# The first chunk's inverse: its store and its reload move from SyncE's DMA queue to ScalarE's

## The chip, the cores and the metric

The kernel runs on one core of a Trainium2 chip. The metric is the device time of one execution in microseconds (us), the median of several runs. A core has five engines that each work through their own instruction queue in order: TensorE (PE, matrix products; PEld is its weight load), VectorE (DVE), ScalarE (ACT), GpSimd (POOL) and SyncE (SP, which here only issues DMA transfers). A DMA transfer can be issued by more than one engine; the profile calls the issue SPq or ACTq, and lists the packets of SyncE's queue as q1 and those of ScalarE's as q10.

## The reference, cut to what matters

```python
def _attn_ref(q, k, v, beta):          # batch 4, heads 8, sequence 768, head size 48
    k_n = k / (np.linalg.norm(k, axis=-1, keepdims=True) + 1e-06)
    for t in range(S):
        kt, vt, bt = k_n[:, :, t], v[:, :, t], beta[:, :, t, None]
        y[:, :, t] = np.einsum('bhd,bhde->bhe', q[:, :, t], state)
        v_old = np.einsum('bhde,bhd->bhe', state, kt)
        state = state + bt[:, :, :, None] * np.einsum('bhd,bhe->bhde', kt, vt - v_old)

x = attention output as 3072 tokens x 384
h = x @ w_in                            # 384 x 2048
g = where(h >= 1, h, where(h <= -1, 0, (h + 1) ** 2 / 4))
x = g @ w_out                           # 2048 x 384
xn = x / rms(x) * rms_g                 # second block: gate and value 384 x 1536, silu, out
out = (silu(xn @ w_gate) * (xn @ w_val)) @ w_out2
```

All of it is in 32-bit floats.

## The kernel before, in words

The attention is computed in 12 chunks of 64 steps, with two pairs of batches per chunk. In a chunk the step-by-step recurrence becomes a triangular system, and its inverse is needed before the chunk's output. Chunk 0 has a short way of its own, `inv0` (lines 455 to 508): the Gram products `gk`, scaled, are stored to DRAM (`scr_a`, L449) and read back as 16 x 16 blocks, one block per partition (`nt`, eight loads, L473); VectorE inverts all blocks at once in 15 steps (`tmp` L479 and `x` L485) and copies the result, transposed, into `nt` (L487). That tile is stored to the DRAM scratch `scr` (L490) and reloaded in another layout as `c` (L493). VectorE multiplies `c` by a mask of coefficients `m` (L497) into the block-diagonal tile `dt` (L503). TensorE multiplies with `dt` (`tr`, L644 and L652) and goes on with products of 32 x 32 blocks (`tr`, L666).

Beside this start-up the kernel prepares the weights of the first block. They arrive as 64-bit floats in 32 tiles of 128 x 3,072 bytes (`wst`, issued by SyncE at L265). ScalarE converts each (`dy` L275, `da` L276), VectorE combines (`dy` L286, `da` L287, `w` L297), ScalarE copies the high part (`w` L300), TensorE forms the low part in three products (`wlo`, L315 to L317; the second and the third read the two parts of `w`), and ScalarE or VectorE copies it out (L320, L322). Later chunks use another routine, `inverse`, on GpSimd, whose store `scr_x` (L541) ScalarE issues. The two big blocks of matrix products (`hps`, `acc`, `gv`, L736 to L738) fill the rest of the time.

The order of all instructions is fixed when the program is built. Each step is a generator that yields stages (`S(engine, cost, needs, buffers)`), and a planner (`Flow`) picks which one is written next, by estimated times. The stages of the store and the reload are declared as stages of SyncE, so the planner places them by its clock for SyncE, and the instruction is written at that place in the program. Each engine then runs its own instructions in the order in which they were written. Where the planner expects TensorE to be idle, it writes a fixed number of small products (`warm`, L866). A DMA signals its end on one of eight semaphores, taken in turn; an instruction that uses the same one again waits for the transfer before.

Of the kernel before, what the change touches and what calls it, by code (L numbers as in the profile page):

```python
# [160 lines left out]
def kernel_body(  # L161
# [10 lines left out]
    nc = tc.nc  # L172
# [179 lines left out]
    inv = {}  # L352
# [5 lines left out]
    def bc(t, n):  # L358
        return t.unsqueeze(2).to_broadcast([t.shape[0], t.shape[1], n])

    def early(shape, name):
        n = int(np.prod(shape[1:]))
        t = wp.tile([128, 2, DM], F32R, name=name, tag="w")
        t = t.rearrange("p a b -> p (a b)").bitcast(F32)[:, 0:n]
        return t.rearrange("p (a b) -> p a b", b=shape[-1]) if len(shape) == 3 else t

    def half(b):
        return slice(64 * b, 64 * b + 64)
# [86 lines left out]
    def inv0():  # L455
        yield S("POOL", 2.0, (), ("tx", "tx", "z", "z", "wp"))
        off["m"] = moff = early([128, C], "moff")
        nc.gpsimd.memset(moff, -1.0)
        nc.gpsimd.memset(mdiag, -1.0)
        for b in range(2):  # L460
            for t, base, pat, cm in ((moff, -16, [[-16, 4], [0, 16]], 1), (mdiag, 0, [[-16, 4]], 1), (mdiag, 15, [[16, 4]], -1)):
                nc.gpsimd.affine_select(
                    out=t[half(b)], in_=t[half(b)], compare_op=ALU.is_ge, fill=0.0, base=base, pattern=pat, channel_multiplier=cm
                )
        x = p2.tile([128, 16, 16], F32, name="x0", tag="tx")
        nc.gpsimd.memset(x, 0.0)
        nc.gpsimd.affine_select(out=x, in_=x, compare_op=ALU.not_equal, fill=1.0, base=0, pattern=[[1, 16], [-1, 16]], channel_multiplier=0)
        yield S("SP", (5, 2.4), [("a_gram", 0, 2), ("a_gram", 1, 2)])
        nt = p2.tile([128, 16, 16], F32, name="nt0", tag="g21")
        for k in range(8):  # L470
            o, c = 16 * k, 16 * (k % 4)
            eng = nc.scalar if k in (1, 3, 5) else nc.sync
            eng.dma_start(out=nt[o:o + 16], in_=scr_a[0][o:o + 16, :, :, c:c + 16].rearrange("t u h s -> (u h) t s"))  # L473
        tmp = p2.tile([128, 64], F32, name="tmp0", tag="tx")
        for j in range(15):
            n, m = 15 - j, j + 1
            yield S("DVE", 0.37 + n * m * 2 / 960)
            tv = tmp[:, 0:n * m].rearrange("p (a b) -> p a b", a=n)
            nc.vector.tensor_tensor(  # L479
                out=tv,  # L480
                in0=nt[:, m:16, j:m].to_broadcast([128, n, m]),
                in1=x[:, j:m, 0:m].to_broadcast([128, n, m]),
                op=ALU.mult,
            )
            nc.vector.tensor_tensor(out=x[:, m:16, 0:m], in0=x[:, m:16, 0:m], in1=tv, op=ALU.add)  # L485
        yield S("DVE", 0.35)
        nc.vector.tensor_copy(nt, x.rearrange("p t s -> p s t"))  # L487
        yield S("SP", (1, 1.5))
        scr = dram.tile([16, 8, 2, H, 16], F32, name="scr_0", tag="scr_0")
        nc.sync.dma_start(out=scr.rearrange("s x u h t -> (x u h) s t"), in_=nt)  # L490
        yield S("SP", (1, 0.5))
        inv["c"] = p2.tile([128, 2 * H, 16], F32, name="c0", tag="z")
        nc.sync.dma_start(out=inv["c"], in_=scr.rearrange("s x u h t -> x s (u h t)"))  # L493
        yield S("DVE", 0.8, ["consts2"], ("x2",))
        m = p2.tile([128, 2 * H, 4], F32, name="m0", tag="g21")
        nn = coef[0][1].rearrange("p u h -> p (u h)")
        nc.vector.tensor_tensor(out=m, in0=bc(nn, 4), in1=mdiag.unsqueeze(1).to_broadcast([128, 2 * H, 4]), op=ALU.mult)  # L497
        inv[0] = x2p.tile([128, 2 * H, 4, 16], F32, name="dt", tag="x2")
        for u in range(2):
            us = slice(H * u, H * u + H)  # L500
            if u:
                yield S("DVE", 0.6, (), (), ("tx", "tx", "z", "z"))
            nc.vector.tensor_tensor(  # L503
                out=inv[0][:, us],
                in0=inv["c"][:, us].unsqueeze(2).to_broadcast([128, H, 4, 16]),
                in1=m[:, us].unsqueeze(3).to_broadcast([128, H, 4, 16]),
                op=ALU.mult,
            )
# [311 lines left out]
    def m1_rms(j):  # L820
# [38 lines left out]
        s=2, w_=2, g=4, acc=1, x2=1, ea=2,  # L859
# [13 lines left out]
    with tc.manual_schedule():  # L873
# [7 lines left out]
        fl.free["PE"] = 6.9  # L881
        fl.idle = spin
        fl.add(PG[0] + 6, inv0)
        for g, us in enumerate(GRP):
            p0 = PG[g]
# [189 lines left out]
```

## Time and profile before

| | |
|---|---|
| time, median of 3 runs | 1153.7 us (1152.92 to 1155.39) |
| profiled execution | 1154.3 us, span 1152.4 us |
| TensorE busy | 1107.5 us (96%) |
| VectorE busy | 661.8 us (57%) |
| ScalarE busy | 569.9 us (49%) |
| GpSimd busy | 286.3 us (25%) |
| SyncE's queue q1 | 141,536 packets, 132.31 MB |
| ScalarE's queue q10 | 23,440 packets, 2.93 MB |

The busy shares are averages over stages with different limits. The transfers that the change touches lie in the first 50 us, where TensorE runs short groups and warming products, and VectorE and ScalarE prepare weights. A timeline row gives start, length, engine, line and instruction; in brackets stands how long the engine sat idle before it and what ended that. Rows of the chain of waits give the work that the end of the program was traced back to.

### The profile page before, as it was taken

The numbers are of one execution on the slowest core, as the hardware profiler recorded it, in microseconds if no ns is written. First come the engines' busy times: TensorE is split into PE (matmuls) and PEld (weight loads), VectorE is DVE, ScalarE is ACT, GpSimd is POOL, SyncE is SP. The second block draws the span as 40 slices with busy tenths as digits, with TensorE's granted clock in tenths as the row PEclk, the third lists the DMA queues.
The fourth block names the chain that finished last, engine by engine and source line by source line (L and its number), as shares of the span: only waits on it lengthen the run. The fifth ranks groups of instructions, "written<-read, shape, count | busy, mean of one in ns | idle before, by whom it ended". The sixth has DMA issues, their size and how long they took to land.

```text
span 1152.4 us, 27191 instructions
## 1 busy us (share of the span) xinstructions
PE 1107.5 (96%) x11224; PEld 996.4 (86%) x11224; DVE 661.8 (57%) x1337; ACT 569.9 (49%) x1360; POOL 286.3 (25%) x479
## 2 busy tenths in 40 slices
PE   8979999999999999999999999999999999999998
PEld 7857888899998999899999999788888888888887
DVE  6797876786877876785775453443433333333333
ACT  4677877765765767567665464222212122122212
POOL 3282865858348114811000000000000000000000
PEclk9989999999999999999999999999999999999999
DMA  7945587784786556385440564001001010010000
GB/s 219 285 143 138 148 262 197 231 208 153 185 224 185 128 199 181 114 206 172 151 148 2 183 207 167 10 23 37 19 1 46 10 37 19 1 46 10 28 1 28
DMA packets 165099, 136.97 MB, mean 119 GB/s; under 512 B 115056, under 2 KB 126064, under 8 KB 164976
## 3 DMA queue, kind: packets, MB, share of 16 engines
q1 hardware_dynamic: 141536, 132.31, 38.2%
q10 hardware_dynamic: 23440, 2.93, 1.7%
q8 instruction: 88, 1.44, 0.5%
q14 instruction: 35, 0.29, 0.1%
HBM read 100.88 MB, written 34.34 MB: 117 GB/s over the span
## 4 chain that ended last, share of the span: by engine, by line
PE 74%; DVE 11%; ACT 4%; POOL 3%; DMA 3%; issue 2%; SPq 1%; DVEq 0%; POOLq 0%; ACTq 0%
PE acc L736 9%; PE gv L736 8%; PE gv L737 8%; PE gv L738 8%; PE acc L737 8%; PE acc L738 8%; PE hps L736 4%; PE hps L737 4%; PE hps L738 4%; PE gs L623 2%; POOL xi L536 2%; PE px L691 2%; POOL tmp L530 2%; PE tr L678 1%; DVE da L287 1%
## 5 line engine op out<-in xcount | busy, mean ns | idle before, releaser
L752 ACT ACTIVATE xh<-fix 128x512 fp32r<-128x512 f32 x72 | 45.5, 632 | 333.7 <-PE acc L738 328.4
L753 DVE TENSOR_TENSOR xl<-fix,xh 128x512 fp32r<-128x512 f32 x72 | 49.9, 694 | 270.6 <-ACT xh L752 270.6
L736 PE MATMUL hps<-xh,w 128*128 128x256 f32 x576 | 167.5, 291 | 9.9 <-DVE w__1065 L773 2.2
L737 PE MATMUL acc<-g,w 128*128 128x256 f32 x576 | 164.7, 286 | 10.6 <-DVE g L781 10.4
L736 PE MATMUL acc<-g,w 128*128 128x256 f32 x576 | 167.8, 291 | 2.7 <-ACT g L779 2.7
L736 PE MATMUL gv<-fix,w 128*128 128x512 f32 x432 | 168.2, 389 | 0.7 <-DVE fix L978 0.7
L737 PE MATMUL gv<-fix,w 128*128 128x512 f32 x432 | 168.1, 389 | 0.0
L738 PE MATMUL gv<-fix,w 128*128 128x512 f32 x432 | 168.1, 389 | 0.0
L737 PE MATMUL hps<-xl,w 128*128 128x256 f32 x576 | 164.2, 285 | 0.0
L738 PE MATMUL hps<-xh,w 128*128 128x256 f32 x576 | 163.9, 285 | 0.0
L738 PE MATMUL acc<-g,w 128*128 128x256 f32 x576 | 163.5, 284 | 0.0
L769 ACT ACTIVATE s<-hps 128x256 f32<-128x256 f32 x192 | 73.6, 384 | 108.3 <-PE hps L738 104.2
L736 PEld LDWEIGHTS hps<-xh,w 128*128 128x128 f32 x576 | 111.2, 193 | 13.7 <-DVE w__1065 L773 2.6
L737 PEld LDWEIGHTS acc<-g,w 128*128 128x128 f32 x576 | 110.7, 192 | 13.0 <-DVE g L781 12.9
L530 POOL TENSOR_TENSOR tmp<-nt,xi 128x87 f32<-128x87 f32 (+21 forms) x186 | 104.4, 561 | 54.5 <-DMA nt<-scr_a 40.4
L736 PEld LDWEIGHTS acc<-g,w 128*128 128x128 f32 x576 | 110.4, 192 | 6.1 <-ACT g L779 2.9
L536 POOL TENSOR_TENSOR xi<-xi,tmp 128x87 f32<-128x87 f32 (+21 forms) x186 | 110.4, 594 | 14.6
L737 PEld LDWEIGHTS hps<-xl,w 128*128 128x128 f32 x576 | 111.4, 193 | 0.3 <-DVE xl L732 0.3
L738 PEld LDWEIGHTS hps<-xh,w 128*128 128x128 f32 x576 | 111.3, 193 | 0.0
L738 PEld LDWEIGHTS acc<-g,w 128*128 128x128 f32 x576 | 110.7, 192 | 0.0
L770 ACT ACTIVATE s<-s,vhalf 128x256 f32<-128x256 f32 x192 | 97.9, 510 | 6.2
L736 PEld LDWEIGHTS gv<-fix,w 128*128 128x128 f32 x432 | 81.1, 188 | 17.8 <-DVE fix L978 1.1
(747 smaller groups left out, 2156.5 us busy)
## 6 DMA issues: line engine op xcount, KB each, us to landing
wst<-in_w SPq DMA_DIRECT2D x68, 384.0 KB, 4.6
w2d<-wst SPq DMA_DIRECT2D x36, 384.0 KB, 4.1
w<-w2d SPq DMA_DIRECT2D x36, 384.0 KB, 6.0
wsv<-in_w SPq DMA_DIRECT2D x36, 383.5 KB, 5.5
kvb<-in_kv SPq DMA_DIRECT2D x22, 384.0 KB, 5.5
kt<-in_kqT SPq DMA_DIRECT2D x24, 256.0 KB, 4.2
scr_a<-al SPq DMA_DIRECT2D x24, 256.0 KB, 3.9
qs<-in_kqT SPq DMA_DIRECT2D x48, 128.0 KB, 4.3
```

Source lines behind the costliest of these rows:

```text
L287: nc.vector.tensor_scalar(out=a, in0=yf, scalar1=0xFF800000, scalar2=None, op0=ALU.bitwise_and)
L530: nc.gpsimd.tensor_tensor(out=tv, in0=nt[:, m:32, j:m].to_broadcast([w, n, m]), in1=x[:, j:m, 0:m].to_broadcast([w, n, m]), op=ALU.mult,)
L536: nc.gpsimd.tensor_tensor(out=x[:, m:32, 0:m], in0=x[:, m:32, 0:m], in1=tv, op=ALU.add)
L623: nc.tensor.matmul(out=ps[half(b), h, 0:n], lhsT=kt[u][half(1 - b), 4 * k + h, :], rhs=qs[p][half(1 - b), b, 4 * k + h, 0:n], start=True, ...
L691: nc.tensor.matmul(out=ps[half(b), h, 0:D], lhsT=t[:, 0:C], rhs=v, start=True, stop=True)
L736: nc.tensor.matmul(out=out, lhsT=wh, rhs=xh, start=first, stop=False, skip_group_check=shared)
L737: nc.tensor.matmul(out=out, lhsT=wh, rhs=xl, start=False, stop=False, skip_group_check=shared)
L738: nc.tensor.matmul(out=out, lhsT=wl, rhs=xh, start=False, stop=last, skip_group_check=shared)
L752: nc.scalar.activation(out=hi, in_=src, func=ACTF.Copy)
L753: nc.vector.tensor_tensor(out=lo, in0=src, in1=hi.bitcast(F32), op=ALU.subtract)
L769: nc.scalar.activation(out=s, in_=ps, func=IDENTITY_SAT240, scale=240.0)
L770: nc.scalar.activation(out=s, in_=s, func=ACTF.Square, bias=vhalf, scale=1.0 / 480.0)
```

## The change

The two transfers are issued by ScalarE instead of SyncE. The stages keep their declaration as SyncE stages with the same costs, so the planner's order of all other instructions is the same.

```diff
         nc.vector.tensor_copy(nt, x.rearrange("p t s -> p s t"))
         yield S("SP", (1, 1.5))
         scr = dram.tile([16, 8, 2, H, 16], F32, name="scr_0", tag="scr_0")
-        nc.sync.dma_start(out=scr.rearrange("s x u h t -> (x u h) s t"), in_=nt)
+        nc.scalar.dma_start(out=scr.rearrange("s x u h t -> (x u h) s t"), in_=nt)
         yield S("SP", (1, 0.5))
         inv["c"] = p2.tile([128, 2 * H, 16], F32, name="c0", tag="z")
-        nc.sync.dma_start(out=inv["c"], in_=scr.rearrange("s x u h t -> x s (u h t)"))
+        nc.scalar.dma_start(out=inv["c"], in_=scr.rearrange("s x u h t -> x s (u h t)"))
```

On ScalarE's queue the two transfers now stand among the weight conversions, as the difference between the two programs shows (`scr_472` is the scratch, `c_558` the reloaded tile; in brackets what an instruction waits for, where `DMAHW` names a DMA semaphore):

```order
 L275 ACTIVATE dy<-wst 128x384 [waits DMAHW7_49,Activation_49]
 L276 ACTIVATE da_99<-wst 128x384
+L490 DMA scr_472<-nt_289 128x16x16 [waits DMAHW2_49,DMAHW5_49,DMAHW1_49,DMAHW6_49,DMAHW0_49,DVE_49]
 L275 ACTIVATE dy<-wst 128x384 [waits DMAHW0_49,Activation_49]
 L276 ACTIVATE da_100<-wst 128x384
@@ -39,4 +40,5 @@
 L276 ACTIVATE da_102<-wst 128x384
 L397 ACTIVATE n__545<-ss 128x16 [waits DVE_49]
+L493 DMA c_558<-scr_472 128x1x256 [waits DMAHW3_49]
 L300 ACTIVATE w<-dy 128x384 [waits DVE_49]
 L275 ACTIVATE dy<-wst 128x384 [waits DMAHW4_49,Activation_49]
```

The store stands behind the first of a run of four pairs of conversions, the reload behind the small `n_` and ahead of a `w` copy; its wait is for the store's semaphore.

On SyncE's queue, at the same place of the program, the weight loads close up:

```order
 L265 DMA wst<-in_w 128x384 [waits DMAHW2_49]
-L490 DMA scr_472<-nt_289 128x16x16 [waits DMAHW3_49,DVE_49]
 L265 DMA wst<-in_w 128x384 [waits DMAHW4_49]
 L265 DMA wst<-in_w 128x384 [waits DMAHW5_49]
 L265 DMA wst<-in_w 128x384 [waits DMAHW6_49]
-L493 DMA c_558<-scr_472 128x1x256 [waits DMAHW7_49,DMAHW3_49]
 L265 DMA wst<-in_w 128x384 [waits DMAHW0_49]
 L265 DMA wst<-in_w 128x384 [waits DMAHW1_49]
 L265 DMA wst<-in_w 128x384 [waits DMAHW2_49]
-L449 DMA scr_a_557<-al 128x512 [waits DVE_49]
+L449 DMA scr_a_557<-al 128x512 [waits DMAHW3_49,DVE_49]
```

Six loads move ahead of the places where the two transfers stood, and the store of `al` behind them now carries the wait for the semaphore of the moved store. The queues of TensorE, VectorE and GpSimd are the same as before.

## Rows read from the trace of the kernel before

**Rows 1.** Chain of waits, 14 to 62 us: start, length, what

```profile
39.66 0.23 DVE m L497
...
39.91 1.29 DVE dt L503 x2
...
44.86 0.87 PE tr L666 x32
```

**Rows 2.** Waits of SyncE's queue, 10 to 60 us: total, times, longest

```profile
SPq L493 <- DMA scr<-nt: 0.6, 1, 0.6
```

**Rows 3.** Timeline of SyncE's issues: start, length, queue, line, transfer

```profile
23.37 2.07 SPq L265 DMA_DIRECT2D wst<-in_w  x4
29.90 0.38 SPq L490 DMA_DIRECT2D scr<-nt  x1
...
33.91 0.69 SPq L493 DMA_DIRECT2D c<-scr  x1
```

**Rows 4.** Timeline of ScalarE, 28 to 45 us

```profile
30.35 0.55 ACT L275 ACTIVATE dy<-wst 128x384 f32<-128x384 f32 x1
...
34.36 0.22 ACT L397 ACTIVATE n__545<-ss 128x16 f32<-128x16 f32 x1 [0.61 <-DVE ss L391]
34.82 0.53 ACT L300 ACTIVATE w<-dy 128x384 fp32r<-128x384 f32 x1 [0.25 <-DVE dy L286]
```

**Rows 5.** DMA queues, 28.00 to 28.99 us: packets, MB, share of 16 engines

```profile
q1 hardware_dynamic: 145, 0.40, 100.4%
```

**Rows 6.** DMA packets by size, 30.75 to 30.99 us

```profile
DMA packets 113, 0.03 MB, mean 130 GB/s; under 512 B 105, under 2 KB 105, under 8 KB 113
```

**Rows 7.** DMA queues, 171.62 to 172.61 us

```profile
q1 hardware_dynamic: 147, 0.38, 96.5%
q10 hardware_dynamic: 145, 0.02, 11.9%
```

**Rows 8.** Timelines of ScalarE's and SyncE's issues around the second `scr_x` store

```profile
165.62 0.39 ACTq L541 DMA_DIRECT2D scr_x<-nt  x1
...
176.29 0.56 SPq L550 DMA_DIRECT2D tx<-scr_x  x1
```

**Rows 9.** DMA queues, 31.00 to 31.99 us

```profile
q1 hardware_dynamic: 1617, 0.16, 109.9%
```

**Rows 10.** Timeline of TensorE, 36 to 42 us and just before

```profile
35.97 0.81 PE L315 MATMUL wlo<-dy,ident 128*128 128x384 f32 x2
36.33 0.63 PE L316 MATMUL wlo<-w,ineg_r 128*128 128x384 f32 x1
...
36.97 2.84 PE L866 MATMUL warm<-ident 128*128 128x128 f32 x24
40.75 1.13 PE L644 MATMUL tr<-kvb,dt 64*64 64x48 f32 x32 [0.94 <-DVE dt L503]
41.69 0.52 PE L652 MATMUL tr<-dt,off 64*64 64x64 f32 x11
```

**Rows 11.** DMA issues of the whole span: transfer, times, KB, median us to landing

```profile
xn<-xn_d SPq DMA_DIRECT2D x18, 256.0 KB, 2.9
```

**Rows 12.** Timeline of TensorE: idle times of 2.0 to 2.5 us, in brackets

```profile
66.93 0.39 PE L736 MATMUL hps<-xh,w 128*128 128x256 f32 x1 [2.23 <-DVE w__1065 L773]
...
230.81 1.56 PE L623 MATMUL gs<-qs,kt 64*64 64x112 f32 x22 [2.48 <-DVE wt L585]
...
467.62 0.39 PE L736 MATMUL hps<-xh,w 128*128 128x256 f32 x1 [2.04 <-DVE w__7804 L773]
```

**Rows 13.** Stretches: length, busy time per engine, granted TensorE clock, DMA share, GB/s

```profile
68.00:70.00 2.00, 2.00 (x7) 1.39 (x6) 1.97 (x3) 1.00 (x3) 1.76 (x4) 0.51 0.03 11
70.00:72.00 2.00, 2.00 (x9) 1.14 (x10) 1.79 (x4) 1.70 (x4) 1.84 (x3) 0.64 0.00 0
...
232.00:234.00 2.00, 2.00 (x33) 2.00 (x32) 1.91 (x7) 0.01 (x1) 1.93 (x3) 0.50 0.65 103
...
468.00:470.00 2.00, 2.00 (x26) 1.70 (x24) 1.94 (x5) 0.91 (x3) 1.76 (x4) 1.00 0.98 301
```

## The prediction

> **What bounds the kernel now.** I read the chain of waits first, because it says which work the end hangs on. Over the whole span it is mostly TensorE, but in the first hundred microseconds it runs through VectorE's queue and then through short TensorE groups; the store and the reload stand in that part. The reader is to see in [rows 1] that `dt`, the instruction that uses the reloaded tile, starts at 39.91 us right behind `m` (39.66 us for 0.23 us): VectorE did not stop for the reload. So the reload is not late today, and an earlier reload buys nothing there. Four microseconds further on the chain is on TensorE (`tr` at 44.86 us), and TensorE is what I follow below.
>
> Then the waits of SyncE's queue and its issues. SyncE stood 0.6 us in front of the reload, until the store had landed [rows 2]. The store went out at 29.90 us; the reload at 33.91 us, which is therefore when the store had landed: 4.0 us [rows 3]. In front of the store SyncE stood from 25.44 us (four loads from 23.37 us, 2.07 us) to 29.90 us, for `nt`. Three weight loads were issued between the two transfers and three behind the reload.
>
> **Part 1, SyncE loses two waits.** The six weight loads no longer stand behind the store and the reload. The next ones may go from 25.4 us on [rows 3], as their own semaphores allow, instead of from 30.3 us, behind the store. Nothing on the chain waits for them: ScalarE takes the first of them only after the tile at 34.82 us [rows 4], and VectorE behind it runs without a stop [rows 1]. Value on the path: 0. But it fills the DMA engines at the very time of the store. In the trace the store's own small packets begin at about 30.75 us (105 of 113 packets in that quarter are under 512 B), so the older loads have drained by then [rows 6]. A saturated queue moved 0.40 MB in a microsecond [rows 5]; six loads of 128 x 3,072 B are 2.36 MB, so SyncE's queue now stays full for another 5.9 us, to about 36.6 us.
>
> **Part 2, the store on ScalarE's DMA queue.** ScalarE reaches it behind the second conversion, at 30.35 us, half a microsecond later than SyncE did, and `nt` is ready. The issue itself costs ScalarE some 0.4 us (the store took 0.38 us on SyncE [rows 3]), which lies in idle time: the conversions end well before `n_` at 34.36 us, and that one waits for VectorE [rows 4]. What matters is how the two queues share the DMA engines. The trace has such a stretch: between 171.62 and 172.61 us SyncE's queue (q1) was loaded with weight loads, and ScalarE's queue (q10) with the 128-byte packets of a `scr_x` store. q1 moved 147 packets and q10 145, one for one, whatever their size [rows 7]. That store was issued at 165.62 us, and the first transfer that needs it went out at 176.29 us [rows 8].
>
> The store is 128 x 16 runs of 64 B, 2,048 packets. Its first packets come about 1 us after its issue (0.85 us before, 29.90 to 30.75 us [rows 3, 6]), at 31.4 us. Up to 36.6 us, when the loads end, it gets one packet for each of theirs: 5.2 us x 145 = 750 packets. The other 1,300 then go at 1,617 per us [rows 9], 0.8 us, to 37.4 us. From the end of the bulk to the landing it was 1.8 us before (2,048 packets from 30.8 us at that rate end at 32.1 us; landed at 33.91 us). So it lands at about 39.2 us instead of 33.9 us. The bounds: 34.4 us if the store takes the 4.0 us it took, and 41.0 us, 30.36 + 10.7 us, if it takes what the store of [rows 8] took until its first user. I take 39.2 us, since the one-for-one row is the nearest to six loads in flight.
>
> **Part 3, the reload waits at the head of ScalarE's queue.** This is the new wait, and it is where I expect the loss. The reload stands behind `n_` (34.36 us) and in front of the `w` copy (34.82 us [rows 4]); everything ScalarE does is queued behind it: that copy, two pairs of conversions, the `wlo` copy, the two `z` copies. TensorE waits for the `w` copy: of the three matrix products into `wlo` the second (36.33 us) reads it [rows 10]. The reload goes at 39.2 us, takes 0.4 us to issue, and the copy starts at 39.6 instead of 34.82 us. It lasts 0.53 us, so the product can start at 40.15 instead of 36.33 us, 3.8 us late. Behind it stand 24 warming products in fixed order, which ended with 0.94 us to spare before `tr` [rows 10]: `tr` is 2.9 us late. The groups behind `tr` start 0.94 us apart by the length that its first one shows (40.75 to 41.69 us), the fourth would be through at 44.5 us, and the next `tr` began at 44.86 us [rows 1]: 0.4 us of cover. That leaves 2.5 us.
>
> Is the reload itself later than that? It landed by 39.91 us, 6.0 us after its issue at the latest [rows 1, 3]. With SyncE's queue drained I take 2.9 us, the nearest load in an otherwise quiet queue [rows 11]: landing at 42.1 us, `dt` 2.2 us late, half of it 0.7 us later still ahead of `tr` at 43.6 us. TensorE's path is the longer one.
>
> SyncE's next store of `al` also gains a wait, for the semaphore that the moved store counts on. It cannot leave before the moved store has landed, but then it meets an empty queue, which gives some of that back; it feeds GpSimd's first inverse, not the chain of [rows 1], and I put it at 0.
>
> **Part 4, the clock of TensorE.** The wait opens a gap on TensorE from about 36.6 us (end of the first `wlo` product) to 40.15 us: 3.5 us. Gaps of 2.23 and 2.48 us were followed by half clock, one of 2.04 us was not [rows 12]. After the first, the granted clock was 0.51 and 0.64 over two stretches of 2 us: 1.96 and 1.44 us at 1.2 GHz, 3.4 us in all; after the second it was 0.50, after the gap of 2.04 us it was 1.00 [rows 13]. Here such a stretch would cover the second `wlo` product, the third and the 24 warming ones, some 3.5 us of work at full clock, so it costs half its length, 1.7 us.
>
> **Sum.** 2.5 + 1.7 = 4.2 us. The chain downstream has no place where a fixed shift is absorbed (a wait on a transfer there is for one issued late too), so I carry it whole. The profiled execution took 1154.3 us around a span of 1152.4 us; that is 0.6 us above the median of 1153.7 us. 1154.3 + 4.2 = 1158.5 us for a profiled run, 1157.9 us for the median.
>
> **Rivals.**
> *No half clock.* TensorE was busy all the time before this gap, and the gap of 2.04 us passed. Then 2.5 us: 1156.2 us, just over 0.2%.
> *A second low stretch* after the first, as TensorE's later groups also wait on each other: another 1.7 us, 1159.6 us.
> *The store is not held up.* ScalarE would have its answer by 34.4 us, before the reload's turn comes, the copy would be 0.4 us late, inside the cover; 1153.7 us, no difference. For it speaks that the reload has only 128 long rows and the store is small; against it [rows 7]. It decides where the store lands: the `w` copy may be late by 1.0 us (TensorE came to it only at 36.33 us, the copy was done at 35.35 us) and by the 0.94 us of the warming products, so up to a landing at about 36.3 us nothing is lost, and the 0.4 us of cover takes that to 36.7 us. From there each microsecond costs one. The Trainium skill, page "DMA: Bandwidth & Descriptors", section "Issuing engines are not separate DMA queues", says that transfers issued by different engines run on the same 16 DMA engines and that another issuer saves only the time of issuing. By that rule alone the move would be worth nothing, 1153.7 us; [rows 7] show the sharing but also that the queue in which a small-packet store stands decides what it is interleaved with.
> *Faster.* The half-clock stretches of [rows 12, 13] hang on short gaps, and loads that come sooner might close two of them: 2 x 1.7 us, 1150.3 us without the loss of part 3. Nothing in the trace says that those gaps wait for loads: VectorE ends all three of [rows 12].
>
> **How the numbers follow.** Forecast 0.48; no half clock 0.18; a second low stretch 0.07; store not held up 0.21; faster 0.06. 0.2% is 2.3 us, about what a measurement of this kernel can tell from no change. Slower by more: all of the forecast, the second stretch, and half of the no-half-clock case, 0.64. Within: the store not held up and the other half, 0.30. Faster 0.06. The range goes from 1153.0 us, which takes in the store that is not held up, to 1159.5 us, which leaves out the second stretch and the gains.
>
> **What would show it.** In the profile after: the reload issued on ScalarE near 39 us (before 36.7 us would refute part 3, and the landing estimate of part 2 with it); q1 and q10 moving equal packet counts from 32 to 36 us; a gap of over 3 us on TensorE before the second `wlo` product; a granted clock below 1.00 around 40 to 44 us; `tr` near 45 us instead of 40.75 us. The prediction is wrong if the store's packets get more than their one-for-one share, or if a shift of some microseconds at 45 us has vanished by the time the TensorE-bound part begins.

## The result and the profile after

With the two transfers on ScalarE's queue the kernel takes 1160.6 us, the median of 7 runs (1159.75 to 1165.4). The kernel before took 1155.5 us on the same occasions (7 runs, 1152.92 to 1157.23). The ratio is 1.0054, with an interval from 1.0036 to 1.0071: slower by half a per cent. The profiled execution took 1160.43 us around a span of 1158.1 us; the one before was 1154.3 around 1152.4 us. The span has grown by 5.7 us.

The page of the kernel after, its busy times and its two DMA queues (packets, MB, share of 16 engines):

```profile
PE 1112.5 (96%) x11224; PEld 1001.7 (86%) x11224; DVE 660.0 (57%) x1337; ACT 569.5 (49%) x1360; POOL 288.3 (25%) x479
...
q1 hardware_dynamic: 139336, 132.05, 38.1%
q10 hardware_dynamic: 25640, 3.20, 1.9%
```

About 2,200 packets have moved from q1 to q10, the store's and the reload's; the engines have the same number of instructions as before, and all busy times but TensorE's stand within 2 us of those before. So what has changed is when things run. The chain of waits, 30 to 60 us, in order of time (start, length, what), shows it at once:

```profile
29.50 10.18 DMA scr<-nt
...
39.70 1.21 ACTq L493
...
40.95 0.53 ACT w L300
...
41.53 0.69 PE wlo L316
...
42.54 4.19 PE warm L866 x24
```

Before, this stretch of the chain ran over VectorE's `m` and `dt` [rows 1]. Now it begins with ten microseconds of the store, goes over the issue of the reload on ScalarE, the `w` copy behind it, and the `wlo` product that reads the copy.

SyncE's issues, 20 to 60 us (start, length, queue, line, transfer), to be read beside [rows 3]:

```profile
22.68 10.36 SPq L265 DMA_DIRECT2D wst<-in_w  x10
39.74 0.80 SPq L449 DMA_DIRECT2D scr_a<-al  x2
```

Four loads, the store, three loads, the reload and three loads have become ten loads in one piece. The store of `al`, which now counts on the moved store's semaphore, goes right after that one has landed (39.70 us).

ScalarE, 28 to 50 us, to be read beside [rows 4]:

```profile
29.50 0.39 ACTq L490 DMA_DIRECT2D scr<-nt  x1
...
39.70 1.21 ACTq L493 DMA_DIRECT2D c<-scr  x1
40.95 0.52 ACT L300 ACTIVATE w<-dy 128x384 fp32r<-128x384 f32 x1 [6.77 <-issue]
```

The store is issued 0.4 us earlier than before (29.50 for 29.90 us) and lands 5.8 us later (39.70 for 33.91 us). From the end of the small `n_` (33.96 us for 0.22 us) ScalarE stands at the reload, at the head of its queue, for 5.5 us, and the `w` copy comes 6.1 us late (40.95 for 34.82 us). The 6.77 us in brackets are put down to the engine's own issuing; they hold the reload's wait for the store and its 1.21 us of issue.

TensorE, 28 to 62 us, beside [rows 1, 10], and VectorE's `dt`:

```profile
35.57 0.81 PE L315 MATMUL wlo<-dy,ident 128*128 128x384 f32 x2
41.53 0.69 PE L316 MATMUL wlo<-w,ineg_r 128*128 128x384 f32 x1 [5.14 <-ACT w L300]
...
42.33 4.39 PE L866 MATMUL warm<-ident 128*128 128x128 f32 x24
46.65 1.14 PE L644 MATMUL tr<-kvb,dt 64*64 64x48 f32 x32
...
50.53 0.87 PE L666 MATMUL tr<-z,y 32*32 32x48 f32 x32
```

```profile
43.40 1.29 DVE L503 TENSOR_TENSOR dt<-c,m 128x512 f32<-128x512 f32 x2 [3.92 <-DMA c<-scr]
```

TensorE was idle for 5.14 us in front of L316, and the warming products then took 4.39 us instead of 2.84 us. VectorE waited 3.92 us for the reloaded tile, which it had not done before. The first of the 32 x 32 products (L666) starts at 50.53 instead of 44.86 us: 5.67 us, the growth of the span. Stretches of two microseconds (the last three columns are granted clock, DMA share and GB/s) tell why the warming products are long:

```profile
38.00:40.00 2.00, 0.00 (x0) 0.00 (x0) 1.41 (x4) 0.00 (x0) 0.00 (x0) 0.69 0.04 6
40.00:42.00 2.00, 0.47 (x1) 0.47 (x2) 0.00 (x0) 1.05 (x3) 0.00 (x0) 0.50 0.70 214
42.00:44.00 2.00, 2.00 (x10) 2.00 (x10) 0.60 (x1) 1.87 (x5) 0.00 (x0) 0.50 0.97 346
44.00:46.00 2.00, 2.00 (x13) 2.00 (x12) 1.93 (x5) 0.92 (x3) 0.00 (x0) 0.61 0.91 264
```

The clock fell to its lower level (1.2 GHz) while TensorE was idle and was back at 2.4 GHz shortly before `tr`. It fell once more from about 56 us on, which the part on the prediction comes back to.

Last, the packets of the two queues, one answer per microsecond. From 33.00 to 33.99 us:

```profile
q1 hardware_dynamic: 129, 0.35, 87.9%
q10 hardware_dynamic: 228, 0.01, 15.8%
```

From 34.00 to 34.99 us:

```profile
q10 hardware_dynamic: 1342, 0.09, 93.1%
q1 hardware_dynamic: 57, 0.14, 45.9%
```

From 36.00 to 36.99 us:

```profile
q1 hardware_dynamic: 138, 0.37, 94.9%
q10 hardware_dynamic: 50, 0.00, 3.5%
```

The microsecond before these, 32.00 to 32.99 us, has 153 packets of q1 and none of q10, although the store was issued at 29.50 us. So the store does three things in turn: it waits 3.6 us without a packet (the first one is at 33.12 us), it sends most of its 2,048 packets in a burst in which q1 falls to less than half of its rate, and its remainder trickles out beside the loads until 38.9 us.

### The profile page after: what moved, and what is told of

It is laid out like the page before. It is cut to its first block, busy times and chain, and to the rows that moved or that the text cites. A ratio compares the mean times of both kernels' runs of the same rounds, so it can differ in the third digit from the quotient of the medians.

```text
span 1158.1 us, 27193 instructions
## 1 busy us (share of the span) xinstructions
PE 1112.5 (96%) x11224; PEld 1001.7 (86%) x11224; DVE 660.0 (57%) x1337; ACT 569.5 (49%) x1360; POOL 288.3 (25%) x479
## 4 chain that ended last, share of the span: by engine, by line
PE 75%; DVE 12%; ACT 6%; DMA 3%; issue 2%; SPq 1%; POOL 0%; ACTq 0%; DVEq 0%; POOLq 0%
PE acc L736 9%; PE acc L737 8%; PE gv L736 8%; PE gv L738 8%; PE gv L737 8%; PE acc L738 8%; PE hps L736 5%; PE hps L737 4%; PE hps L738 4%; PE gs L623 2%; PE tr L678 1%; ACT al L445 1%; PE px L691 1%; DVE da L287 1%; DVE g L781 1%
## 5 line engine op out<-in xcount | busy, mean ns | idle before, releaser
L736 PE MATMUL hps<-xh,w 128*128 128x256 f32 x576 | 167.8, 291 | 9.3 <-DVE w__7804 L773 2.1
L737 PE MATMUL acc<-g,w 128*128 128x256 f32 x576 | 164.8, 286 | 7.8 <-DVE g L781 7.6
L736 PE MATMUL acc<-g,w 128*128 128x256 f32 x576 | 167.7, 291 | 3.0 <-ACT g L779 3.0
L736 PE MATMUL gv<-fix,w 128*128 128x512 f32 x432 | 168.2, 389 | 0.7 <-DVE fix L978 0.7
L737 PE MATMUL gv<-fix,w 128*128 128x512 f32 x432 | 168.1, 389 | 0.0
L737 PE MATMUL hps<-xl,w 128*128 128x256 f32 x576 | 164.2, 285 | 0.0
L736 PEld LDWEIGHTS hps<-xh,w 128*128 128x128 f32 x576 | 111.4, 193 | 13.4 <-DVE w__7804 L773 2.4
L737 PEld LDWEIGHTS acc<-g,w 128*128 128x128 f32 x576 | 110.8, 192 | 10.0 <-DVE g L781 9.7
L536 POOL TENSOR_TENSOR xi<-xi,tmp 128x87 f32<-128x87 f32 (+21 forms) x186 | 113.0, 608 | 14.6
L736 PEld LDWEIGHTS acc<-g,w 128*128 128x128 f32 x576 | 110.4, 192 | 6.4 <-ACT g L779 3.2
L737 PEld LDWEIGHTS hps<-xl,w 128*128 128x128 f32 x576 | 111.6, 194 | 0.0
L736 PEld LDWEIGHTS gv<-fix,w 128*128 128x128 f32 x432 | 81.1, 188 | 17.8 <-DVE fix L978 1.1
```

The source lines that it names most:

```text
L536: nc.gpsimd.tensor_tensor(out=x[:, m:32, 0:m], in0=x[:, m:32, 0:m], in1=tv, op=ALU.add)
L736: nc.tensor.matmul(out=out, lhsT=wh, rhs=xh, start=first, stop=False, skip_group_check=shared)
L737: nc.tensor.matmul(out=out, lhsT=wh, rhs=xl, start=False, stop=False, skip_group_check=shared)
```

## The experiments

Each edit is against the kernel after. The ratio is against the kernel before, on the same chip and occasion. The time at which `nt` is finished varies by about 2 us from run to run, so durations are compared rather than clock times; L666 is the first 32 x 32 product, which starts 15.4 us behind the start of the `nt` copy in the kernel before (29.49 to 44.86 us). Where an expectation names a theory by a letter, that letter stands for what the expectation says with it. The order is that of the questions: which of the two transfers costs, on which path, what holds the store up, and what the clock adds.

**The store alone.** The reload is back on SyncE's queue.

```
-        nc.scalar.dma_start(out=inv["c"], in_=scr.rearrange("s x u h t -> x s (u h t)"))
+        nc.sync.dma_start(out=inv["c"], in_=scr.rearrange("s x u h t -> x s (u h t)"))
```

> Only the store goes to ScalarE's queue; SyncE keeps the reload, and with it stops behind three more weight loads instead of six until the store has landed. Theory A (the loss comes from six loads ahead of the store, and is passed on because ScalarE stands at the reload): the store has three loads ahead (1.18 MB, 3 us), lands near 36.5 us instead of 39.7 us, the reload lands by 40 us, `dt` starts within 1 us of 39.9 us, ScalarE's `w` copy is on time at about 34.8 us, no gap over 2 us on TensorE at 36 to 42 us; time as before, ratio 0.999 to 1.002. Theory L (a store issued by ScalarE is slow in itself): the store still lands near 39.7 us, `dt` is 3 to 4 us late, ratio to before 1.003 to 1.005.

Measured: 1.0019, interval 1.0004 to 1.0033. ScalarE issued the store at 30.37 us. SyncE's loads and reload, then TensorE's `tr`:

```profile
24.21 5.21 SPq L265 DMA_DIRECT2D wst<-in_w  x7
...
37.93 0.70 SPq L493 DMA_DIRECT2D c<-scr  x1
```

```profile
41.79 1.23 PE L644 MATMUL tr<-kvb,dt 64*64 64x48 f32 x32 [2.22 <-DVE dt L503]
```

Seven loads are now ahead of the reload instead of ten, since SyncE itself stops at it. The store took 7.6 us (30.37 to 37.93 us) instead of 4.0, its first packet came at 33.74 us, and the `w` copy was on time (34.79 us). Counted from the `nt` copy (29.25 us), `dt` and `tr` were 1.3 us late, and the gap of 2.22 us in front of `tr`, which I had not expected, was followed by half clock; L666 came 2.6 us late. Moving the store alone is enough to starve it. The loss is less than half, but two things differ from the kernel after: ScalarE does not stand at the reload, and three loads fewer run ahead. The reload from GpSimd, below, shows that the first alone does not save the time.

**The reload alone.** The store is back on SyncE's queue.

```
-        nc.scalar.dma_start(out=scr.rearrange("s x u h t -> (x u h) s t"), in_=nt)
+        nc.sync.dma_start(out=scr.rearrange("s x u h t -> (x u h) s t"), in_=nt)
```

> Only the reload goes to ScalarE's queue; the store stays on SyncE, where it holds the loads back until `nt` is written. Theory A: the store lands at 33.9 us as before, before ScalarE comes to the reload at 34.4 us; ScalarE loses only the issue (0.7 to 1.2 us), inside the cover of 1.9 us, TensorE has no gap; ratio 0.999 to 1.001. Rival (a transfer issued by ScalarE costs its engine more than the issue): the `w` copy starts later than 36.7 us and `tr` is late by what goes beyond; ratio above 1.002.

Measured: 1.0032, 1.0019 to 1.0046. The reload on ScalarE, then TensorE's `tr`:

```profile
34.22 1.19 ACTq L493 DMA_DIRECT2D c<-scr  x1
```

```profile
43.25 1.95 PE L644 MATMUL tr<-kvb,dt 64*64 64x48 f32 x32 [3.64 <-DVE dt L503]
```

That the time would be as before fell. The store was as quick as ever and the reload was issued at 34.22 us, as early as on SyncE; the `w` copy at 35.46 us was within its cover. But six loads now went out of SyncE's queue in one piece from 30.12 us on, around the reload, and it sent its first packet at 38.34 us, 4.1 us after its issue, and landed 8.2 us after it. VectorE waited 2.73 us for it, TensorE 3.64 us for VectorE. So the reload starves in ScalarE's queue as the store does.

**The reload from GpSimd.** GpSimd is idle here, so nothing stands behind the reload.

```
-        nc.scalar.dma_start(out=inv["c"], in_=scr.rearrange("s x u h t -> x s (u h t)"))
+        nc.gpsimd.dma_start(out=inv["c"], in_=scr.rearrange("s x u h t -> x s (u h t)"))
```

> Store on ScalarE's queue as in the changed kernel, reload on GpSimd's queue, which has nothing to do from 22 to 48 us: the store is as late as in the changed kernel (39 to 40 us) but ScalarE does not stand in front of the reload. Theory A (ScalarE's standing is what costs): the `w` copy is on time near 34.5 us, the `wlo` products and the warming products behind them too, TensorE's gap shrinks to the wait for `dt` (from about 39.5 to 44 us); `tr` 3 to 4 us late instead of 5.9 us, ratio 1.002 to 1.004. Theory B (the late reload alone makes the loss): `dt` and `tr` as late as in the changed kernel, ratio 1.005.

Measured: 1.0052, 1.0032 to 1.0071. GpSimd's issue and TensorE's `tr`:

```profile
41.70 0.79 POOL L493 DMA_DIRECT2D c<-scr  x1 [20.32 <-DMA scr<-nt]
```

```profile
47.16 1.94 PE L644 MATMUL tr<-kvb,dt 64*64 64x48 f32 x32 [7.40 <-DVE dt L503]
```

ScalarE was free: the `w` copy came at 35.72 us and L316 on time. The loss was the same. The store took 11.3 us, `dt` waited 6.27 us for the reload, and TensorE stood 7.40 us for `dt`. So freeing ScalarE does not save the time: the path over the reload and `dt` alone is as long.

**The reload later in ScalarE's queue.** It is written one stage later, behind the `w` copy; both transfers stay on ScalarE.

```
-        nc.scalar.dma_start(out=inv["c"], in_=scr.rearrange("s x u h t -> x s (u h t)"))
         yield S("DVE", 0.8, ["consts2"], ("x2",))
+        nc.scalar.dma_start(out=inv["c"], in_=scr.rearrange("s x u h t -> x s (u h t)"))
```

> Both transfers on ScalarE's queue as in the changed kernel, loads ahead as there, but the reload is written six ScalarE instructions further on, behind the `w` copy that TensorE waits for. So ScalarE does not stand in front of that copy, and the reload still goes out when the store lands, near 39.7 us. Theory B (the late reload alone costs as much as ScalarE's standing): the `wlo` products are on time at 36.3 us, `dt` starts near 43.4 us as in the changed kernel, TensorE waits from 39.6 to 44.2 us and falls to half clock there; the first 32 x 32 `tr` near 50 us, ratio 1.004 to 1.0055. Theory of the forecast (ScalarE's standing is the longer path, the reload alone costs 2.2 us and no half clock): ratio 1.001 to 1.0025.

Measured: 1.0055, 1.0036 to 1.0074. ScalarE, then TensorE:

```profile
33.29 0.52 ACT L300 ACTIVATE w<-dy 128x384 fp32r<-128x384 f32 x1
...
39.10 1.21 ACTq L494 DMA_DIRECT2D c<-scr  x1
```

```profile
43.22 1.95 PE L644 MATMUL tr<-kvb,dt 64*64 64x48 f32 x32 [4.93 <-DVE dt L503]
```

This says the same without another engine: the copy and L316 (34.80 us) are on time, and TensorE's gap has moved from L316 to `tr`, where it is 4.93 us long and is followed by half clock in `tr` itself (1.95 us where the kernel before took 1.13). Two paths of nearly equal length start at the store's landing; taking one away leaves the other.

**The loads held until `nt` is finished.** SyncE stores 1 KB of `nt` to a spare place where the store used to stand, so it stops there until `nt` is finished, as in the kernel before, and then issues its loads. The 1 KB is an extra transfer.

```
         nc.scalar.dma_start(out=scr.rearrange("s x u h t -> (x u h) s t"), in_=nt)
+        nc.sync.dma_start(out=dram.tile([1, 16, 16], F32, name="hold", tag="hold"), in_=nt[0:1])
```

> Both transfers on ScalarE's queue as in the changed kernel, but SyncE first stores 1 KB of `nt` to a scratch of its own at the place where the whole store stood, so that the six loads cannot run ahead of the store. Theory A1 (the store lost because its packets share the DMA engines one for one with loads in flight): five or six loads are issued within 3 us of the store, so it shares with them and lands at 37 to 38.5 us; ScalarE stands at the reload until then, ratio 1.002 to 1.004. Theory A2 (the store's packets only come after the loads that were issued before it): nothing is ahead of it now, it lands at 34 to 35 us, no gap on TensorE, ratio 0.999 to 1.001. Theory L (ScalarE's issue itself): as in the changed kernel, 39.7 us, ratio 1.005.

Measured: 1.0036, 1.0017 to 1.0054. SyncE's loads behind the extra store, and ScalarE's reload:

```profile
30.57 9.63 SPq L265 DMA_DIRECT2D wst<-in_w  x6
```

```profile
39.88 1.20 ACTq L493 DMA_DIRECT2D c<-scr  x1
```

The packets from 31.00 to 31.49 us, and from 36.00 to 36.49 us:

```profile
q10 hardware_dynamic: 389, 0.02, 50.6%
q1 hardware_dynamic: 17, 0.04, 25.4%
```

```profile
q1 hardware_dynamic: 71, 0.21, 105.3%
q10 hardware_dynamic: 8, 0.00, 1.1%
```

With the earlier loads nearly through (84 packets of q1 from 30.25 to 30.99 us), the store (issued at 30.23 us) sent its first packet 0.9 us later, and over 800 packets before 32 us. Then the loads that were issued right behind it came in, and it landed only at 39.88 us, 9.65 us after its issue. The landing times of theories A1 and A2 did not come out. That of theory L, 39.7 us, did, so this run by itself leaves open that a store issued by ScalarE is slow in itself; the next one settles it. What the packets show is that the store went out at once and slowed when the loads came: loads issued after the store delay it too, by sharing, and for longer than an even one-for-one sharing would.

**The loads held until the store has landed.** Where the store used to stand, SyncE reads 1 KB of the scratch back, and so waits for the store.

```
         nc.scalar.dma_start(out=scr.rearrange("s x u h t -> (x u h) s t"), in_=nt)
+        nc.sync.dma_start(out=dram.tile([1, 256], F32, name="hold", tag="hold"), in_=scr[0:1, 0].rearrange("s u h t -> s (u h t)"))
```

> Both transfers on ScalarE's queue; SyncE reads 1 KB of the scratch back at the place where the store stood, so that it goes on with the loads only when the store has landed. The store then has a quiet queue, the reload has the loads of about 1 us ahead of it and the others behind. Theory A (loads in flight make the two late): the store lands 4.0 us after its issue as it did on SyncE's queue, 33.5 to 34.2 us; ScalarE does not stand, the `w` copy is at 35.5 to 36 us, inside its cover, the second `wlo` product on time at 36.3 us; the reload lands at 38.5 to 41 us, `tr` 0 to 1.5 us late, no or one short low stretch of the clock; ratio 1.000 to 1.003, the upper end if the loads, 3 us later than before, are missed later on. Theory L (ScalarE's issue is slow in itself): store at 38 us or later.

Measured: 1.0043, 1.0028 to 1.0058, more than I had expected. ScalarE's two transfers; then TensorE; then a piece of the chain of waits:

```profile
30.61 0.39 ACTq L490 DMA_DIRECT2D scr<-nt  x1
...
34.67 1.33 ACTq L493 DMA_DIRECT2D c<-scr  x1
```

```profile
40.13 1.14 PE L644 MATMUL tr<-kvb,dt 64*64 64x48 f32 x32 [0.21 <-DVE dt L503]
...
44.25 0.87 PE L666 MATMUL tr<-z,y 32*32 32x48 f32 x32 [0.17 <-DVE y L660]
...
49.22 2.47 PE L666 MATMUL tr<-z,y 32*32 32x48 f32 x64 [2.91 <-ACT z L670]
```

```profile
39.50 7.95 DMA kk<-in_kv
```

This is the cleanest reading of the cause. From ScalarE's queue, with no load in the way, the store took 4.06 us, as on SyncE's (4.0 us, [rows 3]); theory L is refuted. `dt` and `tr` were on time, and L666 came 15.38 us behind the start of the `nt` copy (28.87 to 44.25 us), against 15.37 us before. Up to there the move, with the loads held, costs nothing. The ratio still shows a loss, all of it behind that point: from L666 to the end this kernel took 1115.2 us, the one before 1107.5 us. The chain names a place: a transfer of `kk`, issued behind the six loads that had been held, took 7.95 us (before, it was issued at 38.74 us and ScalarE worked on it from 43.70 us, 5.0 us at the most), and TensorE stood 2.91 us in front of a later L666, which it then ran at half clock (2.47 us; before, 1.42 us). So what protects the store in this way delays what stands behind the loads.

**The loads held twice,** once for `nt` as above, and again where the reload used to stand, until `c` is there (another extra 1 KB).

```
+        nc.sync.dma_start(out=dram.tile([1, 16, 16], F32, name="hold", tag="hold"), in_=nt[0:1])
...
+        nc.sync.dma_start(out=dram.tile([1, 16, 16], F32, name="hold2", tag="hold2"), in_=inv["c"][0:1])
```

> Both transfers on ScalarE's queue, and SyncE held back at both places where they stood: it stores 1 KB of `nt` where the store stood and 1 KB of the reloaded tile where the reload stood. So three loads come behind the store and three only after the reload, nearly as before. Theory A (the loads in flight make the two transfers late, nothing else): the store lands when the three loads are through, near 36 us, the reload near 40 us; the `w` copy is 2.5 us late, 0.6 us beyond its cover, no gap over 2 us on TensorE, `tr` 0.3 to 1 us late, ratio 1.000 to 1.0015. Theory L (a transfer issued by ScalarE is slow in itself): store at 39 to 40 us, ratio 1.004 to 1.006.

Measured: 1.0049, 1.0029 to 1.0069, far more than theory A said. SyncE's loads behind the second hold went out from 39.45 us on. TensorE:

```profile
38.17 0.44 PE L316 MATMUL wlo<-w,ineg_r 128*128 128x384 f32 x1 [2.13 <-ACT w L300]
...
38.63 4.47 PE L866 MATMUL warm<-ident 128*128 128x128 f32 x24
```

With three loads behind the store instead of six it took 6.95 us (29.41 to 36.36 us), between the 4.06 us of no load and the 9.65 us of six. `dt` was on time (39.18 us). The gap in front of L316 was only 2.13 us, and half clock still followed. From L666 to the end this kernel took 1111.7 us where the kernels before and after took 1107.5 and 1107.6 us: some 4 us came in later. That the loads held back cost them is not shown: the kernel after, which holds none, took 1111.4 us for that part when run again.

**The gap filled.** To see the clock's part, 21 more warming products stand between the first and the second product of the group in which TensorE waits (the sixth `wlo`). They change no result. The edit was run on two occasions, on the second beside the kernel after.

```
-        nc.tensor.matmul(out=ps, lhsT=ident, rhs=y.bitcast(F32), start=True, stop=False)
+        nc.tensor.matmul(out=ps, lhsT=ident, rhs=y.bitcast(F32), start=True, stop=False); nwlo.append(0); [nc.tensor.matmul(out=warm[0][:, 0:128], lhsT=ident, rhs=ident, start=True, stop=True) for _ in range(21 * (len(nwlo) == 6))]
```

> The changed kernel with 21 more warming products on TensorE between the first and the second product of the `wlo` group that waits, about 5 us of them, so that TensorE is busy while it waits for the `w` copy. They change no result. Theory C (half clock behind the gap costs 1.6 us, as the product of 5.12 us from the second `wlo` product to `tr` against 3.48 + 0.94 us before says): granted clock 1.00 from 36 to 46 us, `tr` about 3.5 us behind the second `wlo` product, near 45.0 us instead of 46.65 us, the first 32 x 32 `tr` near 48.9 instead of 50.5 us; 1.6 us faster than the changed kernel, ratio to before 1.003 to 1.004. If the clock is no term of the loss: `tr` and time as in the changed kernel, ratio 1.005.

> The changed kernel with 21 more warming products in TensorE's gap, again, beside the changed kernel itself. Theory C (half clock behind the gap costs 1.6 us): 0.001 to 0.002 below the ratio of the changed kernel run beside it; clock 1.00 from 36 to 46 us. If the clock is no term that reaches the end: the same ratio within 0.0005.

> The changed kernel once more, on the same chip and beside the same runs of before as the two others here, to have its ratio with them. All theories: ratio 1.004 to 1.006; reload issued 10 us after the store; half clock around 40 to 45 us.

Measured: 1.0038 (1.0024 to 1.0051) and, on the second occasion, 1.0051 (1.0036 to 1.0065), where the kernel after gave 1.0063 (1.0044 to 1.0082) beside it. TensorE with the gap filled, first occasion:

```profile
42.87 0.44 PE L316 MATMUL wlo<-w,ineg_r 128*128 128x384 f32 x1 [0.82 <-ACT w L300]
...
43.32 2.84 PE L866 MATMUL warm<-ident 128*128 128x128 f32 x24
46.09 1.14 PE L644 MATMUL tr<-kvb,dt 64*64 64x48 f32 x32
```

The clock stayed at 1.00 over this stretch, and from L316 to `tr` it took 3.22 us, on both occasions, where the kernel after took 5.12 us (41.53 to 46.65 us) and 5.97 us when run again. So the half clock behind the gap costs about 2 us, by the trace. In the whole time the filled gap was better by 0.0012 of the kernel's time (1.4 us) where the kernel after ran beside it, and on the first occasion by 0.0016 (1.8 us) against the ratio that the kernel after had on another one. The direction is the same, but the intervals overlap: the times alone do not settle it.

## Why the prediction was right, and where it was wrong

The direction and the chain of waits hold: the reload waits at the head of ScalarE's queue for a store that the loads hold up, TensorE waits for the `w` copy, half clock follows, and the end comes later. The forecast of 1157.9 us was too low: 1160.6 us lies 1.1 us above the end of the range. The step that failed is the lateness of the second `wlo` product (3.8 us forecast, 5.20 us measured), above all the issue of the reload, put at 0.4 us and measured at 1.21 us; as mechanisms, the one-for-one sharing behind the landing time and the plain carry to the end failed too. Of the 2.7 us of error, 1.8 us come from the base: the median of before is 1155.5 us with seven runs, not 1153.7 us with three. The rest, by its own terms:

- **SyncE loses two waits, worth 0:** holds. Ten loads in one piece, and no gain on the chain. The later store of `al` was put at 0 as well; it went out 2.0 us later (39.74 for 37.72 us), and the chain of waits does not run through it.
- **The store on ScalarE's queue, landing at 39.2 us:** the clock time came near (39.70 us), in part by luck: the store took 10.2 us instead of the 8.85 us of the forecast, and was issued 0.85 us earlier than I had assumed. The account of it holds only in part. I had it send its first packets 1 us after the issue and then go one for one with the loads to 36.6 us. It sent nothing for 3.6 us, then 1,342 packets in a microsecond in which the loads moved 57, then a trickle. The equal counts from 32 to 36 us, which were to show it, are not there (1,885 packets of q10, 448 of q1), and the store did get more than its one-for-one share, which the prediction had named as a sign of being wrong. The runs show two effects. Loads issued before go first: the first packet came 3.0 to 4.1 us after the issue in the eight runs in which loads had been issued just ahead, 0.9 to 1.1 us in the three that held the loads. And loads issued behind it share with it: 4.06, 6.95 and 9.65 us for none, three and six of them.
- **The `w` copy at 39.6 us, L316 3.8 us late:** this is the term of the sum that failed. L316 was 5.20 us late. Of the 1.4 us more, 0.8 us are the issue of the reload, which I took as 0.4 us from the store's issue and which took 1.21 us on ScalarE (0.69 us on SyncE, [rows 3], which was the row to take, and too short as well); 0.5 us are the landing.
- **"TensorE's path is the longer one", the reload alone 2.2 us late:** falls as an account of the cost, since it suggests that without the blocked `w` copy only a small loss would be left. `dt` was 3.5 us late (43.40 us) in the kernel after, and with the `w` copy free (reload from GpSimd, reload later in the queue) TensorE waited 7.40 and 4.93 us for `dt`, and the ratios are 1.0052 and 1.0055. I had taken 2.9 us for the reload, as in a quiet queue (it took up to 3.7 us, 39.70 to 43.40 us), and had not counted that its gap would bring half clock of its own.
- **The half clock, 1.7 us:** holds. L316 to `tr` took 5.12 us; before it was 4.42 us, of which 0.94 us were the spare time (36.33 to 40.75 us). 5.12 − 3.48 = 1.64 us. A gap filled with products gave 3.22 us.
- **Cover and carry:** the 0.94 us hold; of the 0.4 us at the end 0.23 us were found. 5.20 − 0.94 + 1.64 − 0.23 = 5.67 us, which is L666's shift, and the span grew by 5.7 us. From L666 to the end it took 1107.5 us before and 1107.6 us after, and 1107.1 to 1108.2 us in the five experiments that did not hold the loads for the transfers to land and did not fill the gap: a shift there reaches the end nearly whole. (Counted from the `nt` copy, which came 0.4 us earlier in this execution than in the one before, L666's shift is 6.1 us.) The kernel after, run a second time, took 1111.4 us for that part, as the filled gap did (1110.0 and 1110.6 us). In that second run the shift was 7.6 us at L666 and 7.3 us at the `wlo` product of 117.13 us (109.81 us before), so those 4 us came in behind the start-up; what cost them stays open.

One thing happened that the sum does not have. TensorE fell to half clock a second time, from about 56 to 66 us. One stretch of the kernel before, and two of the kernel after (the last three columns are again granted clock, DMA share and GB/s):

```profile
56.00:60.00 4.00, 3.98 (x42) 3.14 (x37) 3.89 (x8) 3.35 (x8) 3.53 (x7) 1.00 1.02 350
```

```profile
56.00:60.00 4.00, 4.00 (x73) 3.57 (x70) 0.00 (x0) 1.85 (x4) 3.53 (x7) 0.50 0.45 139
60.00:64.00 4.00, 4.00 (x73) 3.55 (x69) 0.76 (x2) 1.97 (x5) 3.53 (x7) 0.50 0.01 4
```

That is the rival of a second low stretch, and it made the shift larger: the first product of the first block (`hps`, L736) started 10.3 us late (68.85 for 58.53 us). It then grew smaller where TensorE waits for VectorE: in front of the first `acc` product of L737 the wait was 4.11 us instead of 6.00 us (90.13 for 82.93 us), and at the `wlo` product of 115.73 us (109.81 us before) the shift was 5.9 us. So the sentence that nothing downstream absorbs a fixed shift falls. The sum meets the growth of the span because a second loss was made up again.

Of the other rivals, the store that is not held up is refuted (10.2 us), and so is the one without half clock (0.50 from 40 to 44 us). The Trainium skill, page "DMA: Bandwidth & Descriptors", section "Issuing engines are not separate DMA queues", says that issuing from another engine saves only the time of issuing, as all transfers run on the same 16 engines. The trace agrees on the shared engines (q1 fell from 129 packets in a microsecond to 57 while q10 moved 1,342), but not that nothing else changes: the choice of queue cost 5.7 us of the span here, because it decides what a small transfer waits behind and shares with.

Open: why the first packets wait for the loads issued on the other queue. The profile shows the packets, not what stands ahead of them. No kernel here beats the one before.

## What to carry to other kernels

An empty queue did not make this small transfer faster: its neighbours in the old queue had been kept out of its way by the wait in front of it, and moving it let them go first. Before moving a transfer, list what was queued behind it and will now run ahead of it, and what stands behind it on the new engine; both are prices. Where two paths start at the same late event, freeing one shows nothing until the other is costed too.

## What the runs showed of the hardware that I had not expected

- The first packet of a transfer on ScalarE's queue came 3.6 us after its issue with loads ahead on SyncE's queue (4.1 us for the reload alone), and 0.9 us where the loads were held (until `nt`, and until the store had landed).
- The reload's issue, of 128 rows of 1 KB, took 1.19 to 1.33 us on ScalarE in all its runs, even where the loads had not yet been let go when it began (1.33 us in the run that held them until the store had landed), against 0.69 to 0.70 us on SyncE and 0.79 us on GpSimd.
- Idle times of 2.13 and 2.22 us on TensorE were followed by half clock here, where [rows 12, 13] show one of 2.04 us that was not. The second low stretch of the kernel after, from about 56 us, came behind an idle time of only 0.52 us (in front of L666 at 55.07 us); when the kernel was run again, the same 0.52 us (57.03 us) was not followed by one.
